# Token mixing one tile later, and softmax sums as a 65th column of the values, in a fused attention and mixer kernel

## The chip, the core and the metric

The kernel runs on one core of a Trainium2 chip. The core has five engines that run their own instruction queues: TensorE (PE: matmuls, with weight loads as PEld), VectorE (DVE), ScalarE (ACT), GpSimd (POOL) and SyncE (SP, which issues DMAs). They wait for each other by semaphores. The metric is the device time of one execution in microseconds.

## The reference

The inputs are q, k and v of 8 batches, 8 heads, 576 positions and 64 dimensions, and four weight matrices. Attention has a causal window of 64 positions. Its output x (576 x 512 a batch) goes through token mixing, a residual, channel mixing and another residual:

```
scores = where(0 <= i - j < 64, q @ k.T / 8, -1e9)
attn   = exp(scores - max);  attn = attn / (sum(attn) + 1e-9);  x = attn @ v
h   = relu(x.T @ w_tok1) @ w_tok2          # w_tok1 576x256, w_tok2 256x576
u   = x + h.T
out = u + relu(u @ w_ch1) @ w_ch2          # w_ch1 512x1536, w_ch2 1536x512
```

The weights come in float64 and are converted on the chip.

## The kernel before

The kernel has two stages. The first does attention and token mixing and ends near 284 us; the second does channel mixing in nine chunks of 512 tokens (lines L593 and L629).

The first stage works in 36 tiles, nine for a pair of batches. A tile i has 128 query rows: two blocks of 64, of one batch, or of two batches in the fifth tile of a pair (i % 9 = 4). The program is written out by hand: one loop runs over i from -1 to 36, and an iteration holds work of several tiles, so that what waits for one engine stands beside what another does. In iteration i stand, in this order:

- `pt_transpose(i, 0)`: four PE transposes of the softmax numerators e of half the heads into a PSUM tile pp (L301), and an ACT copy of it to SBUF as pt (L303). In the first four iterations (`early`) the other half follows at once; later it stands after the pieces named below. PSUM has two banks for pp.
- `softmax(i+1, 0)`: on DVE, the mask and the row maximum of the next tile's scores s (L283, L286; from tile 7 on). In the first tiles the mask is put in by PE (L260) and DVE takes only the maximum (L280, L281).
- `recip(i)`: sum + 1e-9, and its reciprocal ri (L321, L322, on DVE).
- `job_finish`: the halves of a converted weight; ACT makes the high half (L91), POOL or DVE the low one (L94).
- `softmax_exp(i+1, 0)`: four ACT exponentials with `accum_out` (L294), each with an instruction that reads the accumulator to give the row sums.
- a piece of token mixing's second matrix product, `tok2` (L393 transposes of x, L400 six matmuls), into the one bank "up", copied by ACT as u (L405).
- `job_convert_a`: DVE bit operations that turn float64 words to float32 (L185 to L188), in iterations whose number isn't divisible by three (and in the first six).
- `pt_transpose(i, 1)`, `softmax(i+1, 1)`.
- `tok1(n)` for the tiles n that a plan lists: the first token-mixing product h (L358), from three matmuls for each of two output halves, with x split in a high and a low part, xhi (ACT, L91) and xlo (POOL, L94). In the fifth tile of a pair the parts are made by half the rows (L338, L339). When a batch is complete, `finish_h` makes hhi (ACT, L369) and hlo (DVE, L370), and lists eight pieces.
- `softmax_exp(i+1, 1)`, `job_convert_b` (DVE, L197 to L200, and POOL, L202).
- `av(i)`: 32 matmuls xp = pt.T @ v (L313), and `norm(i)`: x = xp * ri (DVE, L327).
- `qk(i+2)`: scores of the tile after the next (L266), another piece, then `split_x` for tiles that the plan lists for the next iteration and that were not split yet.

The plan lists tile 0 in iteration 2, tile 1 in 3, tiles 2 and 3 in 4, and from then on tile i-1 in iteration i. So xhi and xlo of a tile are made between its `norm` and the first h matmuls of the next iteration.

PSUM has eight banks of 128 x 512 float32: s 2, pp 2 (tag "pt"), up 1, h 2, xp 1 (tag "av"). In the second stage these tags serve the products gp and op. The two functions of the plan and of the bank choice are in the lines below:

```
m = min(n + (1 if i < TOK1_SLOW else 2), i)          # L458
gp = ps.tile(..., tag=("s", "pt")[ft % 2])           # L589
tag, bufs = (("h", 2), ("av", 1), ("h", 2), ("up", 1))[ct]   # L617
```

Of the kernel before, what the change touches and what calls it, by code (L numbers as in the profile page):

```python
# [10 lines left out]
F32 = mybir.dt.float32  # L11
# [8 lines left out]

B, H, S, D = 8, 8, 576, 64
C = H * D
P = 128
BLK = 64
NBLK = S // BLK
# [2 lines left out]
NT = NPAIR * TPP  # L28
# [12 lines left out]


JOBS = {i: 1 if i < 6 or i % 3 else 0 for i in range(-1, 37)}
PIECES = {32: (1, 0), 33: (1, 0), 34: (1, 0), 35: (3, 0), 36: (2, 1)}

TOK1_FROM, TOK1_SLOW, TOK2_FROM = 2, 4, 7

N_PE, N_EARLY = 7, 4

# [25 lines left out]
def mixer_kernel(ctx: ExitStack, tc: tile.TileContext, qh, kh, vh, wt1, wt2, wc1, wc2, out):  # L75
# [37 lines left out]
    with ExitStack() as actx:  # L113
# [19 lines left out]
            loaded[i] = [qr, None]  # L133

        def load_v(i):
            vt = pq.tile([P, 2, H, D], F32, name=f"v{i}", tag="v", bufs=3)
            nc.sync.dma_start(vt, vh[i])
            loaded[i][1] = vt

# [129 lines left out]

        def softmax(i, u):  # L270
            if u == 0:
                st[i] = (pa.tile([P, H], F32, name=f"nm{i}", tag="nm", bufs=3),
                         pa.tile([P, H], F32, name=f"sum{i}", tag="sum", bufs=3))
            nm, sm = st[i]
            mk = mask[1 if tile_blocks(i)[0][1] == 0 else 0]
            e = pa.tile([P, 4, P], F32, name=f"e{i}_{u}", tag="e", bufs=4)
            e_sb[i, u] = e
            nmu = nm.rearrange("p (j u) -> p j u", u=2)[:, :, u]
            if i < N_PE:
                nc.vector.tensor_reduce(out=nmu, in_=s_ps[i, u], axis=AX.X, op=ALU.max, negate=True)  # L280
                nc.vector.tensor_scalar_mul(nmu, nmu, scale)  # L281
                return
            nc.vector.scalar_tensor_tensor(  # L283
                out=e, in0=s_ps.pop((i, u)), scalar=scale,
                in1=mk.unsqueeze(1).to_broadcast([P, 4, P]), op0=ALU.mult, op1=ALU.add)
            nc.vector.tensor_reduce(out=nmu, in_=e, axis=AX.X, op=ALU.max, negate=True)  # L286

        def softmax_exp(i, u):
            e = e_sb[i, u]
            nm, sm = st[i]  # L290
            src, by = (s_ps.pop((i, u)), scale) if i < N_PE else (e, 1.0)
            for h in range(4):
                g = 2 * h + u
                nc.scalar.activation(e[:, h], src[:, h], AF.Exp, bias=nm[:, g:g + 1], scale=by,  # L294
                                     accum_out=sm[:, g:g + 1])

        def pt_transpose(i, u):
            pp = ps.tile([P, 4, P], F32, name=f"pp{i}_{u}", tag="pt")
            e = e_sb.pop((i, u))
            for h in range(4):  # L300
                nc.tensor.transpose(pp[:, h], e[:, h], ident)  # L301
            pt = pa.tile([P, 4, P], F32, name=f"pt{i}_{u}", tag="ptsb", bufs=4)
            nc.scalar.copy(pt, pp)  # L303
            return pt
# [2 lines left out]

        def av(i, pts):
            vt = loaded.pop(i)[1]
            xp = ps.tile([P, H, D], F32, name=f"xp{i}", tag="av", bufs=1)  # L310
            for h in [*range(0, H, 2), *range(1, H, 2)]:
                for half in range(2):
                    nc.tensor.matmul(xp[half * BLK:(half + 1) * BLK, h],  # L313
                                     pts[h % 2][:, h // 2, half * BLK:(half + 1) * BLK],
                                     vt[:, half, h], start=True, stop=True)
            return xp

        def recip(i):
            _, sm = st.pop(i)
            ri = pa.tile([P, H], F32, name=f"ri{i}", tag="ri", bufs=2)  # L320
            nc.vector.tensor_scalar_add(ri, sm, 1e-9)  # L321
            nc.vector.reciprocal(ri, ri)  # L322
            return ri

        def norm(i, xp, ri):
            x = pa.tile([P, H, D], F32, name=f"x{i}", tag="x", bufs=12)
            nc.vector.tensor_mul(x, xp, ri.unsqueeze(2).to_broadcast([P, H, D]))  # L327
# [85 lines left out]
        def store_u():  # L413
            while stores:
                us, g0, n = stores.pop(0)
                a = 0
                while a < n:
# [2 lines left out]
                    (nc.sync if g0 < (B - 1) * S - 320 else nc.scalar).dma_start(u_dram[j][:, :, o:o + m], us[:, :, a:a + m])  # L420
                    a += m

        def tok1(i):
            p, t = divmod(i, TPP)
            b0, b1 = 2 * p, 2 * p + 1
            if t < 4:
                tok1_part(i, b0, full, t, t == 0, False)
            elif t == 4:
                tok1_part(i, b0, top, 4, False, True)
                finish_h(b0)  # L430
            else:
                if t == 5:
                    tok1_part(i - 1, b1, bottom, 4, True, False)
                tok1_part(i, b1, full, t - 5, False, t == 8)
                if t == 8:
                    finish_h(b1)

        def run_pieces(k):
            for _ in range(min(k, len(pieces))):
# [15 lines left out]
        load_v(1)  # L455
        tok1_plan, n = {}, 0
        for i in range(TOK1_FROM, NT + 1):
            m = min(n + (1 if i < TOK1_SLOW else 2), i)  # L458
            tok1_plan[i] = range(n, m)
            n = m  # L460
        qk(0)
        for i in range(-1, NT + 1):
            if 0 <= i and i + 2 < NT:
                load_v(i + 2)
            if 3 <= i + 3 < NT:
                load_q(i + 3)
            if i + 4 < NT:
                load_k(i + 4)
            store_u()
            n_jobs = JOBS[i]  # L470
            if i == NT - 1:
                up_tags += [("s", 2), ("pt", 2)]
# [36 lines left out]
            if i + 1 < NT:  # L509
                softmax_exp(i + 1, 1)  # L510
            for _ in range(n_jobs):
                job_convert_b()
            if 0 <= i < NT:
                xp = av(i, pts)
                if i + 1 < N_EARLY:
                    normed = [(i, xp, ri)]
# [22 lines left out]
    with ExitStack() as bctx:  # L539
# [45 lines left out]
        for j in range(NCHUNK):  # L585
            uf, uhi, ulo = ul.pop(j)
            g = []
            for ft in range(NFT):
                gp = ps.tile([P, CHUNK], F32, name=f"gp{j}_{ft}", tag=("s", "pt")[ft % 2])  # L589
                k = 0  # L590
                for ct in range(NCT):
                    for w, x in ((w1hi, uhi), (w1hi, ulo), (w1lo, uhi)):
# [19 lines left out]
            for ct in range(NCT):  # L612
                if j == 0:
                    for _ in range(7):
                        next(late, None)
                    assert all(n in finished for n in range(23 + 4 * ct, 27 + 4 * ct))
                tag, bufs = (("h", 2), ("av", 1), ("h", 2), ("up", 1))[ct]  # L617

                n_part = LAST_PARTS if j == NCHUNK - 1 and ct == NCT - 1 else 1
                for part in range(n_part):  # L620
                    cols = slice(part * CHUNK // n_part, (part + 1) * CHUNK // n_part)
                    if part:
                        tag, bufs = ("s", "pt")[part % 2], 2
# [47 lines left out]
```

## Time and profile before

| | |
|---|---|
| median of 3 runs | 878.97 us (878.91 to 879.26) |
| the profiled execution | 880.53 us, span 878.7 us, granted clock 0.993 |
| PE busy | 850.6 us (97% of the span) |
| PEld busy | 702.6 us (80%) |
| DVE busy | 378.3 us (43%) |
| ACT busy | 307.5 us (35%) |
| POOL busy | 105.3 us (12%) |
| mean duration of an exp, 128x128 | 396 ns; of the read of its accumulator 193 ns |

Times of the trace are counted from the start of the span. A row of the waits names the engine and the line that waited, and what released it, with the sum in us, the count and the longest. A row of the timeline has its start, its duration, the engine and line, the operation with out<-in, and in brackets the idle time before it. Busy times of PE are modelled: matmuls overlap, so the pace is read from start to start. ACT and DVE are idle for most of the second stage, so their shares of the span say little about the first.

### The profile page before, as it was taken

The page shows a single profiled execution, that of the slowest core. Times are in us where ns is not written, and L with a number is a line of the kernel's source. Part 1 is how long each engine was busy: PE and PEld are TensorE (multiplying, and loading weights), DVE is VectorE, ACT ScalarE, POOL GpSimd, SP SyncE. Part 2 cuts the span into 40 slices and gives each one's busy share as a digit, 9 for nine tenths or more (in the row PEclk, how much of TensorE's full clock was granted, in tenths as well). Part 3 has the DMA queues.
Part 4 walks back from the last instruction along what each step waited for, and adds up shares of the span by engine and source line. Part 5 has one row for each costly group of instructions (what it writes and reads, how often), then busy time and mean ns, then how long its engine had stood idle before and what let it go on. Part 6 is the DMA issues. An engine that isn't in the chain of part 4 may idle for free.

```text
span 878.7 us, 14566 instructions
## 1 busy us (share of the span) xinstructions
PE 850.6 (97%) x6002; PEld 702.6 (80%) x6002; DVE 378.3 (43%) x701; ACT 307.5 (35%) x966; POOL 105.3 (12%) x109
## 2 busy tenths in 40 slices
PE   6889999989989999999999999999999999999998
PEld 4668878868879878888888888888888888888887
DVE  5979878878874795220220220220220220220211
ACT  5778777878875341120120220220220220220200
POOL 3433343433332000000000000000000000000000
PEclk9989999999999999999999999999999999999999
DMA  9566667567535531100100100100100101100001
GB/s 322 195 203 229 200 235 244 183 235 246 182 127 167 182 106 57 60 7 30 60 13 24 60 13 25 60 13 25 60 12 31 54 13 39 46 13 37 0 13 37
DMA packets 39907, 84.69 MB, mean 96 GB/s; under 512 B 5281, under 2 KB 18337, under 8 KB 37921
## 3 DMA queue, kind: packets, MB, share of 16 engines
q1 hardware_dynamic: 37728, 81.93, 27.9%
q10 hardware_dynamic: 2112, 1.84, 0.6%
q8 instruction: 47, 0.77, 0.4%
q14 instruction: 20, 0.16, 0.1%
HBM read 64.09 MB, written 19.66 MB: 95 GB/s over the span
## 4 chain that ended last, share of the span: by engine, by line
PE 83%; DVE 8%; ACT 4%; POOL 2%; issue 2%; DMA 1%; POOLq 0%; SPq 0%; DVEq 0%; ACTq 0%
PE op L629 33%; PE gp L593 30%; PE h L358 5%; PE up L400 4%; PE s L266 4%; PE xp L313 3%; PE up L393 2%; POOL xlo L94 2%; PE pp L301 1%; ACT u L405 1%; DVE r L200 1%; DMA u_dram<-u 1%; DVE c L197 1%; ACT xhi L91 1%; ACT e L294 1%
## 5 line engine op out<-in xcount | busy, mean ns | idle before, releaser
L597 ACT ACTIVATE ghi<-gp 128x512 fp32r<-128x512 f32 x108 | 64.5, 597 | 432.2 <-PE gp L593 431.9
L629 PE MATMUL op<-ghi,w2lo 128*128 128x512 f32 (+1 forms) x444 | 170.9, 385 | 1.9 <-DVE w2lo L94 1.9
L629 PE MATMUL op<-glo,w2hi 128*128 128x512 f32 (+1 forms) x444 | 170.9, 385 | 0.0
L629 PE MATMUL op<-ghi,w2hi 128*128 128x512 f32 (+1 forms) x444 | 170.8, 385 | 0.0
L593 PE MATMUL gp<-ulo,w1hi 128*128 128x512 f32 x432 | 168.1, 389 | 0.0
L593 PE MATMUL gp<-uhi,w1hi 128*128 128x512 f32 x432 | 168.1, 389 | 0.0
L593 PE MATMUL gp<-uhi,w1lo 128*128 128x512 f32 x432 | 168.0, 389 | 0.0
L598 DVE SCALAR_TENSOR_TENSOR glo<-gp,ghi 128x512 fp32r<-128x512 f32 x108 | 74.5, 690 | 187.7 <-ACT ghi L597 187.7
L631 DVE TENSOR_TENSOR uf<-op,uf 128x512 f32<-128x512 f32 (+1 forms) x37 | 25.0, 677 | 243.7 <-PE op L629 243.7
L629 PEld LDWEIGHTS op<-ghi,w2lo 128*128 128x128 f32 x444 | 83.9, 189 | 18.8 <-DVE w2lo L94 2.3
L629 PEld LDWEIGHTS op<-ghi,w2hi 128*128 128x128 f32 x444 | 83.8, 189 | 16.6
L629 PEld LDWEIGHTS op<-glo,w2hi 128*128 128x128 f32 x444 | 83.8, 189 | 16.5
L593 PEld LDWEIGHTS gp<-uhi,w1hi 128*128 128x128 f32 x432 | 81.1, 188 | 16.9
L593 PEld LDWEIGHTS gp<-uhi,w1lo 128*128 128x128 f32 x432 | 81.1, 188 | 16.8
L593 PEld LDWEIGHTS gp<-ulo,w1hi 128*128 128x128 f32 x432 | 81.1, 188 | 16.8
L294 ACT ACTIVATE e<-e,nm 128x128 f32<-128x128 f32 x232 | 90.5, 396 | 8.0 <-DVE nm L286 8.0
L94 POOL TENSOR_TENSOR xlo<-x,xhi 128x512 fp32r<-128x512 f32 x32 | 42.9, 1340 | 66.3 <-ACT xhi L91 66.0
L313 PEld LDWEIGHTS xp<-v,pt 128*64 128x64 f32 x1152 | 37.4, 137 | 16.4 <-ACT pt L303 6.3
L266 PE MATMUL s<-k,q 64*64 64x128 f32 x1152 | 43.7, 287 | 2.4 <-DVE c L197 1.9
L313 PE MATMUL xp<-v,pt 128*64 128x64 f32 x1152 | 43.1, 226 | 2.7 <-ACT pt L303 2.4
L294 ACT ACTIVATION_READ_ACCUMULATOR e<-e,nm 128x1 f32 x232 | 44.8, 193 | 0.0
L303 ACT COPY pt<-pp 128x512 f32<-128x512 f32 x72 | 41.8, 587 | 6.4 <-PE pp L301 6.3
(79 smaller groups left out, 1002.7 us busy)
## 6 DMA issues: line engine op xcount, KB each, us to landing
v<-vh SPq DMA_DIRECT2D x36, 512.0 KB, 3.8
raw<-wc SPq DMA_DIRECT2D x32, 384.0 KB, 4.4
q<-qh SPq DMA_DIRECT2D x36, 256.0 KB, 4.6
k<-kh SPq DMA_DIRECT2D x7, 1280.0 KB, 8.0
out<-uf SPq DMA_DIRECT2D x35, 256.0 KB, 2.3
uf<-u_dram SPq DMA_DIRECT2D x8, 1024.0 KB, 5.6
u_dram<-u SPq DMA_DIRECT2D x7, 512.0 KB, 3.7
k<-kh SPq DMA_DIRECT2D x5, 256.0 KB, 6.2
```

Source lines behind the costliest of these rows:

```text
L94: eng_lo.tensor_sub(lo, src, hi.bitcast(F32))
L266: nc.tensor.matmul(s[u][half * BLK:(half + 1) * BLK, j], qt[r, j, half], kbs[b][r, j, n * BLK:n * BLK + P], start=not on_pe, stop=True, sk ...
L294: nc.scalar.activation(e[:, h], src[:, h], AF.Exp, bias=nm[:, g:g + 1], scale=by, accum_out=sm[:, g:g + 1])
L303: nc.scalar.copy(pt, pp)
L313: nc.tensor.matmul(xp[half * BLK:(half + 1) * BLK, h], pts[h % 2][:, h // 2, half * BLK:(half + 1) * BLK], vt[:, half, h], start=True, sto ...
L358: nc.tensor.matmul(h_ps[b][tt], w[:, o + tt * P:o + (tt + 1) * P], x, start=first and n == 0, stop=last and n == len(combos) - 1)
L400: nc.tensor.matmul(up[:, :n], hx[:, cs], w[:, tt * S + s0:tt * S + s0 + n], start=False, stop=(k == 6), skip_group_check=True)
L593: nc.tensor.matmul(gp, w[:, ct * F + ft * P:ct * F + (ft + 1) * P], x[:, ct], start=(k == 0), stop=(k == 3 * NCT - 1))
L597: nc.scalar.activation(ghi, gp, AF.Relu)
L598: nc.vector.scalar_tensor_tensor(out=glo, in0=gp, scalar=0.0, in1=ghi.bitcast(F32), op0=ALU.max, op1=ALU.subtract)
L629: nc.tensor.matmul(op, w[:, ct, ft], x[:, cols], start=(k == 0), stop=(k == 3 * NFT - 1))
L631: nc.vector.tensor_add(uf[:, ct, cols], op, uf[:, ct, cols])
```

## The change

Two things are changed at once.

The plan of `tok1` lags one tile more: up to iteration 33, iteration i handles tiles up to i-2; in iteration 34 two tiles are done, and from there the plan is as before. The halves of x(i) are thus made in iteration i+1, behind its first pt copy, and used in iteration i+2. `finish_h` is moved from within `tok1` behind `av` and `norm`. One more piece is run in iteration 34.

The row sums no longer come from the accumulator. The host puts v in rows of 66 per head: 64 values, a 1 and a 0. `av` multiplies 65 of them, so column 64 of xp is the row sum. xp takes two PSUM banks, four heads in each. `norm` reads the sums from xp, adds 1e-9, takes the reciprocal and multiplies. For the second xp bank, pp has one bank instead of two. In the second stage gp takes banks of s and h, and op those of av, pt, up and av.

```diff
-PIECES = {32: (1, 0), 33: (1, 0), 34: (1, 0), 35: (3, 0), 36: (2, 1)}
-TOK1_FROM, TOK1_SLOW, TOK2_FROM = 2, 4, 7
+PIECES = {32: (1, 0), 33: (1, 0), 34: (2, 0), 35: (3, 0), 36: (2, 1)}
+TOK1_FROM, TOK1_SLOW, TOK1_CATCH_UP, TOK2_FROM = 2, 4, 34, 7
...
-            vt = pq.tile([P, 2, H, D], F32, name=f"v{i}", tag="v", bufs=3)
+            vt = pq.tile([P, 2, H, DV], F32, name=f"v{i}", tag="v", bufs=3)
...
-                nc.scalar.activation(e[:, h], src[:, h], AF.Exp, bias=nm[:, g:g + 1], scale=by,
-                                     accum_out=sm[:, g:g + 1])
+                nc.scalar.activation(e[:, h], src[:, h], AF.Exp, bias=nm[:, g:g + 1], scale=by)
...
-            pp = ps.tile([P, 4, P], F32, name=f"pp{i}_{u}", tag="pt")
+            pp = ps.tile([P, 4, P], F32, name=f"pp{i}_{u}", tag="pt", bufs=1)
...
-            xp = ps.tile([P, H, D], F32, name=f"xp{i}", tag="av", bufs=1)
+            xp = ps.tile([P, 2, CHUNK], F32, name=f"xp{i}", tag="av", bufs=1)
+            xp = xp[:, :, :4 * (D + 1)].rearrange("p u (j d) -> p u j d", j=4)
...
-                    nc.tensor.matmul(xp[half * BLK:(half + 1) * BLK, h],
+                    nc.tensor.matmul(xp[half * BLK:(half + 1) * BLK, h % 2, h // 2],
                                      pts[h % 2][:, h // 2, half * BLK:(half + 1) * BLK],
-                                     vt[:, half, h], start=True, stop=True)
+                                     vt[:, half, h, :D + 1], start=True, stop=True)
...
-        def recip(i):
-            _, sm = st.pop(i)
-            ri = pa.tile([P, H], F32, name=f"ri{i}", tag="ri", bufs=2)
-            nc.vector.tensor_scalar_add(ri, sm, 1e-9)
+        def norm(i, xp):
+            ri = pa.tile([P, 2, 4], F32, name=f"ri{i}", tag="ri", bufs=2)
+            nc.vector.tensor_scalar_add(ri, xp[:, :, :, D], 1e-9)
             nc.vector.reciprocal(ri, ri)
-            nc.vector.tensor_mul(x, xp, ri.unsqueeze(2).to_broadcast([P, H, D]))
+            nc.vector.tensor_mul(x.rearrange("p (j u) d -> p u j d", u=2), xp[:, :, :, :D],
+                                 ri.unsqueeze(3).to_broadcast([P, 2, 4, D]))
...
-                finish_h(b0)
+                to_finish_h.append(b0)
...
-            m = min(n + (1 if i < TOK1_SLOW else 2), i)
+            m = min(n + (1 if i < TOK1_SLOW else 2), i - (i < TOK1_CATCH_UP))
...
-            if 0 <= i < NT:
-                ri = recip(i)
...
-                    norm(i, xp, ri)
+                    norm(i, xp)
+            while to_finish_h:
+                finish_h(to_finish_h.pop(0))
...
-                gp = ps.tile([P, CHUNK], F32, name=f"gp{j}_{ft}", tag=("s", "pt")[ft % 2])
+                gp = ps.tile([P, CHUNK], F32, name=f"gp{j}_{ft}", tag=("s", "h")[ft % 2])
...
-                tag, bufs = (("h", 2), ("av", 1), ("h", 2), ("up", 1))[ct]
+                tag, bufs = (("av", 1), ("pt", 1), ("up", 1), ("av", 1))[ct]
```

What it does to the order shows in tile 22. ScalarE's queue before, from the cast of x(21) to the exponentials of the second half (the numbers behind names are those of buffers, e_0 and e_1 the halves of tile 23):

```order
L91 CAST xhi_2692<-x_2661 128x512
L303 COPY pt_0_2705<-pp_0_2700 128x512
L294 ACTIVATE e_0_2709,sum_2708<-e_0_2709,nm_2707 128x128 x4
L405 COPY u_1_2622<-up_1_2_2719 128x320
L303 COPY pt_1_2739<-pp_1_2734 128x512
L294 ACTIVATE e_1_2741,sum_2708<-e_1_2741,nm_2707 128x128 x4
```

And now, the same stretch of ScalarE's queue:

```order
L304 COPY pt_0_2649<-pp_0_2644 128x512
L94 CAST xhi_2655<-x_2609 128x512
L296 ACTIVATE e_0_2652<-e_0_2652,nm_2651 128x128 x4
L405 COPY u_1_2673<-up_1_0_2663 128x320
L304 COPY pt_1_2684<-pp_1_2679 128x512
L296 ACTIVATE e_1_2686<-e_1_2686,nm_2651 128x128 x4
```

The cast of x(21) stands behind the first pt copy instead of ahead of it, and the exponentials have no sums. VectorE's queue before, around `norm(21)`:

```order
L286 TENSOR_REDUCE nm_2598<-e_1_2631 128x4
L327 TENSOR_TENSOR x_2661<-xp_2644,ri_2603 128x512
L283 SCALAR_TENSOR_TENSOR e_0_2709<-s_0_2663,mask_89 128x512
L286 TENSOR_REDUCE nm_2707<-e_0_2709 128x4
L321 TENSOR_SCALAR ri_2712<-sum_2599 128x8
L322 RECIPROCAL ri_2712<-ri_2712 128x8
```

And now:

```order
L288 TENSOR_REDUCE nm_2545<-e_1_2576 128x4
L323 TENSOR_SCALAR ri_2606<-xp_2589 128x8
L324 RECIPROCAL ri_2606<-ri_2606 128x8
L326 TENSOR_TENSOR x_2609<-xp_2589,ri_2606 128x2x4x64
L285 SCALAR_TENSOR_TENSOR e_0_2652<-s_0_2611,mask_89 128x512
```

The sum and its reciprocal stand directly ahead of the product x, and read xp. On TensorE, the iteration with four h matmuls and no piece between the transposes is 24 (and 15) now; it was 23 (and 32):

```order
L302 MATMUL pp_0_2887<-ident,e_0_2772 128x128 x4
L302 MATMUL pp_1_2908<-ident,e_1_2809 128x128 x4
L358 MATMUL h_0_2464<-xhi_2777,t1hi 128x512
L358 MATMUL h_0_2464<-xhi_2777,t1z 128x512
L358 MATMUL h_1_2465<-xhi_2777,t1hi 128x512
L358 MATMUL h_1_2465<-xhi_2777,t1z 128x512
L316 MATMUL xp_2926<-v_2639,pt_0_2892 64x65 x8
L316 MATMUL xp_2926<-v_2639,pt_1_2913 64x65 x8
```

The two groups of transposes pp stand next to each other there, and share one bank; the values' matmuls stream 65 columns.

More of the change, by code (lines that the diff above doesn't have):

```diff
@@ L22 @@
 C = H * D
+DV = D + 2
 P = 128
@@ L271, in softmax @@
             if u == 0:
-                st[i] = (pa.tile([P, H], F32, name=f"nm{i}", tag="nm", bufs=3),
-                         pa.tile([P, H], F32, name=f"sum{i}", tag="sum", bufs=3))
-            nm, sm = st[i]
+                st[i] = pa.tile([P, H], F32, name=f"nm{i}", tag="nm", bufs=3)
+            nm = st[i]
             mk = mask[1 if tile_blocks(i)[0][1] == 0 else 0]
@@ L289, in softmax_exp @@
             e = e_sb[i, u]
-            nm, sm = st[i]
+            nm = st.pop(i) if u else st[i]
             src, by = (s_ps.pop((i, u)), scale) if i < N_PE else (e, 1.0)
@@ L421, in store_u @@
                     a += m
+        to_finish_h = []
         def tok1(i):
@@ L435, in tok1 @@
                 if t == 8:
-                    finish_h(b1)
+                    to_finish_h.append(b1)
         def run_pieces(k):
@@ L471, in mixer_kernel @@
             if i == NT - 1:
-                up_tags += [("s", 2), ("pt", 2)]
+                up_tags += [("s", 2), ("pt", 1)]
             have = len(pieces)
@@ L515, in mixer_kernel @@
                 if i + 1 < N_EARLY:
-                    normed = [(i, xp, ri)]
+                    normed = [(i, xp)]
                 else:
-                    norm(i, xp, ri)
+                    norm(i, xp)
+            while to_finish_h:
+                finish_h(to_finish_h.pop(0))
             if i + 2 < NT:
@@ L622, in mixer_kernel @@
                     if part:
-                        tag, bufs = ("s", "pt")[part % 2], 2
+                        tag, bufs = "s", 2
                     op = ps.tile([P, CHUNK], F32, name=f"op{j}_{ct}_{part}", tag=tag, bufs=bufs)[:, cols]
@@ L648 @@
     vw = np.stack([vb[bi, ji], vb[bi, ji + 1]], 2).reshape(NT, 2, P, H, D)
-    vh = vw.transpose(0, 2, 1, 3, 4)
+    vh = np.zeros((NT, P, 2, H, DV), v.dtype)
+    vh[..., :D], vh[..., D] = vw.transpose(0, 2, 1, 3, 4), 1
     wt1, wt2, wc1, wc2 = (np.ascontiguousarray(inputs["moe_w_" + n]).view(np.int64)
```

2 lines of the change are left out of this document (removed).

## The prediction

> **What bounds the kernel now.** I read the table of windows first, then the queue waits of TensorE's weight loads, then one tile in order of time. The windows (columns: busy us of PE, PEld, DVE, ACT, POOL, each with its count; granted clock, DMA share, GB/s):
>
> ```profile
> 0.00:50.00 50.00, 38.08 (x510) 27.52 (x510) 36.61 (x85) 34.24 (x134) 21.96 (x38) 1.00 0.77 272
> 50.00:100.00 50.00, 47.47 (x605) 39.42 (x604) 43.61 (x83) 38.44 (x147) 17.94 (x16) 0.93 0.60 199
> 150.00:200.00 50.00, 46.42 (x640) 37.83 (x639) 41.65 (x79) 39.22 (x151) 19.83 (x17) 1.00 0.61 204
> 400.00:878.00 478.00, 475.31 (x2131) 394.85 (x2130) 93.55 (x140) 62.66 (x108) 0.00 (x0) 1.00 0.09 31
> ```
>
> From 400 us on TensorE never rests (475.31 of 478), and the change leaves that stage its instructions. What can move is the attention stage, up to about 284 us. In its middle PE is 93% busy (46.42 of 50), DVE 83%, ACT 78%: PE leads, and small stalls inside each tile are all there is to win. The first 50 us are different: PE 76%, DVE 73% of a stretch that also has the start in it. The stalls from 60 to 255 us (27 tiles, 6 to 32):
>
> ```profile
> 60.00:255.00 195.00, 186.10 (x2504) 153.43 (x2501) 161.63 (x308) 154.07 (x580) 75.11 (x64) 1.00 0.65 218
> PEld h L358 <- POOL xlo L94: 8.0, 17, 1.2
> PEld up L393 <- ACT u L405: 6.3, 22, 0.3
> PEld h L358 <- POOL xhi L339: 4.4, 3, 2.0
> PEld xp L313 <- ACT pt L303: 4.3, 11, 0.9
> PEld h L358 <- ACT xhi L91: 0.8, 2, 0.4
> ```
>
> Token mixing (h) waits 13.2 us (8.0 + 4.4 + 0.8) for the halves of x, which POOL makes; attention times values (xp) waits 4.3 us for the copied transposes. The up wait, 0.3 us a tile, is the one PSUM bank of token mixing's second half. Tile 22 in time:
>
> ```profile
> 170.46 0.60 PE L301 MATMUL pp<-ident,e 128*128 128x128 f32 x4
> 170.63 0.16 DVE L321 TENSOR_SCALAR ri<-sum 128x8 f32<-128x8 f32 x1
> 170.98 0.62 ACT L91 CAST xhi<-x 128x512 fp32r<-128x512 f32 x1
> 171.50 0.59 ACT L303 COPY pt<-pp 128x512 f32<-128x512 f32 x1
> 171.68 1.52 POOL L94 TENSOR_TENSOR xlo<-x,xhi 128x512 fp32r<-128x512 f32 x1 [5.08 <-ACT xhi L91]
> 171.98 0.41 ACT L294 ACTIVATE e<-e,nm 128x128 f32<-128x128 f32 x1
> 172.41 0.60 PE L301 MATMUL pp<-ident,e 128*128 128x128 f32 x4
> 172.76 0.48 PE L358 MATMUL h<-xhi,t1hi 128*128 128x512 f32 x1
> 173.25 0.50 PE L358 MATMUL h<-xlo,t1hi 128*128 128x512 f32 x1
> 173.82 0.39 PE L358 MATMUL h<-xhi,t1hi 128*128 128x512 f32 x1
> 174.05 0.39 PE L358 MATMUL h<-xlo,t1hi 128*128 128x512 f32 x1
> 174.60 1.01 PEld L313 LDWEIGHTS xp<-v,pt 128*64 128x64 f32 x32 [0.35 <-ACT pt L303]
> ```
>
> The second matmul of h starts 0.49 us after the first, where 0.23 is the pace (173.82 to 174.05), since xlo ends at 173.20.
>
> **The change, part by part.** *Two tiles behind.* From tile 4 on, the halves of x(i) are made in iteration i+1, and used in i+2; xlo has a tile's time (some 7 us) more. All 13.2 us of waits go: −13.2. Nothing takes their place on the h matmuls, since even behind both ACT casts and a POOL pass of 1.5 us xlo is done in the iteration before.
>
> *Softmax sums.* The read of the accumulator goes from ScalarE:
>
> ```profile
> L294 ACT ACTIVATE e<-e,nm 128x128 f32<-128x128 f32 x232 | 90.5, 396 | 8.0 <-DVE nm L286 8.0
> L294 ACT ACTIVATION_READ_ACCUMULATOR e<-e,nm 128x1 f32 x232 | 44.8, 193 | 0.0
> L313 PE MATMUL xp<-v,pt 128*64 128x64 f32 x1152 | 43.1, 226 | 2.7 <-ACT pt L303 2.4
> L321 DVE TENSOR_SCALAR ri<-sum 128x8 f32<-128x8 f32 x36 | 11.5, 321 | 0.0
> L322 DVE RECIPROCAL ri<-ri 128x8 f32<-128x8 f32 x36 | 7.3, 203 | 1.2
> ```
>
> Now one exp and its read take 0.39 us from start to start. No row shows exps without reads; the spacing is at least 0.20 (396 − 193 ns) and at most 0.39. In tile 22 two ACT operations back to back overlap by 0.10 us (xhi starts at 170.98, lasts 0.62, and pt starts at 171.50), so I take 0.30: 0.36 us less for four exps. The cast of x, however, moves from ahead of the first copy pt to behind it, 0.52 us in front of the exps and the second pt. So the second pt comes no earlier in tiles with both casts and earlier in the others: of the 4.3 us of xp waits I count half, −2.2. The Trainium skill, "ScalarE: Activation LUTs", section "What ACT_TABLE_LOAD costs", gives an ACTIVATE with a pointer bias 280 ns + 0.833 N, overlapping the next by 93 ns: an estimate of 0.29 us at N = 128. By it the sum would stay as it is, since ACT is not the bound.
>
> *The 65th column.* 1152 matmuls of 43.1 us stream 65 columns for 64: +0.7 (43.1/64). No row has an odd count; the bounds are 0 and, were they to cost double, the 1.08 us of a tile's 32 matmuls again (39 us in all, a rival).
>
> *Reciprocal behind the values.* The same two DVE instructions now wait for xp and stand ahead of x, 0.36 us (0.16 + 0.20, where nothing holds them). Behind them on DVE stands the next e from s, which today waits 0.33 us for PE anyway (the third row is for the next part):
>
> ```profile
> 175.80 0.69 DVE L327 TENSOR_TENSOR x<-xp,ri 128x512 f32<-128x512 f32 x1 [0.91 <-PE xp L313]
> 176.82 0.69 DVE L283 SCALAR_TENSOR_TENSOR e<-s,mask 128x512 f32<-128x512 f32 x1 [0.33 <-PE s L266]
> 177.98 1.04 PE L301 MATMUL pp<-ident,e 128*128 128x128 f32 x8
> ```
>
> So it is covered; only in the last tile, where x feeds the last h directly, +0.4. The wider v is 3% more bytes in a queue at a share of 0.65: 0. finish_h behind the values sends hhi and hlo later, but the next iteration's scores and transposes lie ahead of their use: 0, at most 0.3 in eight places.
>
> *One bank for pp.* The second transposes now wait for the first pt copy. In most tiles a piece (transposes and six matmuls, 1.3 us) lies between: in tile 22 the copy ended 0.32 us ahead (171.50 + 0.59 against 172.41), and with the cast behind it the copy starts some 0.4 us sooner. Tiles 15 and 24 have no piece between: first four transposes 0.60, copy 0.59, hand-overs 0.1 before the second four start, against 0.44 now (eight take 1.04, four 0.60): 0.85 each, +1.7. Before tile 7 there is no piece either, but there DVE is what ends last.
>
> *Before 60 us.* The chain of waits runs through DVE alone from the first to the second row here; at tiles 4 to 6 it goes through ACT, as the rows of the timeline behind them show:
>
> ```profile
> 18.63 0.70 DVE nm L280
> ...
> 37.72 0.61 DVE x L327
> ```
>
> ```profile
> 47.12 1.36 DVE L94 TENSOR_TENSOR t2lo<-w,t2hi 128x384 fp32r<-128x384 f32 x1 [1.30 <-ACT t2hi L91]
> 50.44 0.37 ACT L294 ACTIVATE e<-s,nm 128x128 f32<-128x128 f32 x1 [0.48 <-DVE nm L281]
> 52.00 1.97 PE L266 MATMUL s<-k,q 64*64 64x128 f32 x28 [1.92 <-DVE c L197]
> 56.09 0.63 PE L358 MATMUL h<-xlo,t1z 128*128 128x512 f32 x1
> ```
>
> t2hi now stands ahead of the casts of x, so DVE's 1.30 us goes; four exps of PE's next scores are 0.4 us shorter; ten h matmuls leave tiles 4 to 6, some of them at a lower clock (0.63 us each, not 0.39). Bounds 0 and −6; I take −3, nearest the first two. Those ten matmuls are done later, where PE is the bound: 10 × 0.23 = +2.3.
>
> Sum: −13.2 − 2.2 + 0.7 + 0.4 + 1.7 − 3 + 2.3 = −13.3. The profiled execution took 880.53 us (span 878.7), 1.6 above the median 878.97; 880.5 − 13.3 − 1.6 = 865.6, so 866.
>
> **Rivals.**
> *DVE takes over* (16 in 100, 874). POOL's passes move to where DVE does the second half of a conversion. While POOL works, DVE's operations from SBUF to SBUF stretch:
>
> ```profile
> 264.68 0.60 DVE L321 TENSOR_SCALAR ri<-sum 128x8 f32<-128x8 f32 x1
> 265.55 1.35 POOL L94 TENSOR_TENSOR xlo<-x,xhi 128x512 fp32r<-128x512 f32 x1 [0.29 <-DVE ri L322]
> 265.78 1.33 DVE L187 TENSOR_SCALAR c<-c 128x384 f32<-128x384 f32 x1
> 260.96 0.36 DVE L188 TENSOR_SCALAR c<-c 128x384 int32<-128x384 int32 x1
> ```
>
> 1.33 against 0.36. DVE has (195 − 161.63)/27 = 1.2 us a tile to spare, 0.5 of which the faster PE takes back. One more such stretch (0.97) in the 18 converting tiles leaves 0.3 to 0.5 us a tile exposed, 5 to 8 us: 871 to 874. Against it: the sums in PSUM free L321, and PE needs DVE's results a tile later only. The Trainium skill, "SBUF — State Buffer", section "SBUF: two separate sides", says that VectorE and GpSimd share a port pair as an exclusive lock for the whole instruction; the rows agree.
>
> *The single bank holds PE in every tile* (8 in 100, slower, 889). If ACT starts the first copy late, behind u or a w1hi that waits for POOL, the second transposes wait for it. Fully exposed it is 0.85 us in 27 tiles, +23, so 866 + 23. It decides from 0.5 us a tile (13.3/27); the 0.3 to 0.7 us between copy and transposes speak against it.
>
> *The 65th column is dear* (3 in 100): 866 + 38 = 904. Nothing in the profile speaks for it.
>
> *Everything clears* (13 in 100): all 4.3 us of xp waits, and 6 before 60 us: 858 to 861.
>
> **How the numbers follow.** Forecast 60 in 100, its own range 862 to 870. A measurement tells 0.2% (1.8 us) from no change. Faster: 60 + 13 + 11 of the 16 of DVE = 84; same: 4, DVE's worst case; slower: 8 + 3 + 1 of DVE = 12. The range 858 to 876 leaves out the slower rivals and little else.
>
> **What would show it.** Right: no wait of h on POOL between 60 and 255 us; ACT busy some 25 us lower or more with the reads gone; xp's matmuls at 226 ns still; waits of pp on pt in tiles 15 and 24 alone; tiles near 6.9 us. Wrong: pp waiting on ACT pt in most tiles, xp L316 slower than by 1/64, DVE without idle time, or a lower granted clock than now.

## The result, and the profile after

The changed kernel takes 883.39 us (881.95 to 885.51) where the kernel before takes 879.01 us beside it: a ratio of 1.0047, with a 95% interval of 1.0028 to 1.0065. It is 4.4 us slower, where 13 us less were forecast. The profiled execution took 883.87 us (span 882.0, granted clock 0.994).

The windows of the changed kernel, in the columns explained above:

```profile
0.00:50.00 50.00, 37.67 (x469) 26.77 (x470) 35.05 (x80) 26.57 (x75) 19.85 (x37) 1.00 0.75 251
50.00:100.00 50.00, 45.89 (x597) 37.80 (x599) 42.13 (x78) 33.39 (x92) 17.73 (x15) 0.90 0.62 206
150.00:200.00 50.00, 48.16 (x668) 40.37 (x661) 42.44 (x81) 36.24 (x98) 18.76 (x16) 1.00 0.69 226
400.00:881.00 481.00, 478.58 (x2146) 397.57 (x2144) 93.60 (x140) 62.65 (x108) 0.00 (x0) 1.00 0.09 31
```

In the middle TensorE is busier than before (48.16 of 50, against 46.42), as forecast. The second window is the opposite: 45.89 against 47.47, and a clock of 0.90 against 0.93. Where the time went is read from the starts of the values' matmuls (the first xp of a tile) and of the first gp. I call the stretches by tiles:

| stretch, profiled execution (us) | before | after | difference | forecast |
|---|---|---|---|---|
| start to tile 7 | 64.7 | 69.3 | +4.6 | −3 |
| tile 7 to tile 32 | 183.4 | 178.4 | −4.9 | −10.7 (−13.2 − 2.2 + 1.7 + 0.7 + 2.3) |
| tile 32 to the first gp | 35.3 | 40.7 | +5.4 | +0.4 |
| first gp to the end | 595.3 | 593.6 | −1.7 | 0 |

So a gain is there, less than half of what was forecast, and both ends of the first stage eat it. Some of it is moved work: six h matmuls leave the first stretch, two of them go to the second and four to the third, and one piece goes from the second to the third. With 0.23 us for a matmul and 1.1 us for a piece (53.1 us for 47 of them before, in the table below), 2.0 us of the third stretch's 5.4 are work. The last row has no step of the change behind it: the execution of before that was profiled ran 3.4 us at half clock at 324 us, this one did not. The other choice of banks in the second stage costs nothing there: from its 200th matmul to its 2400th it takes 498.7 us in both profiles.

The waits of the changed kernel from 60 to 255 us, the six largest rows of TensorE on h, xp, pp and s:

```profile
PEld xp L316 <- issue: 6.3, 17, 0.4
...
PEld xp L316 <- ACT pt L304: 3.7, 9, 0.6
...
PEld xp L316 <- DVE c L200: 2.6, 7, 0.4
PE xp L316 <- ACT pt L304: 2.3, 7, 0.4
PEld pp L302 <- ACT pt L304: 1.9, 2, 1.0
PE pp L302 <- ACT pt L304: 1.5, 2, 0.7
```

No row has h waiting for POOL: all of the 13.2 us are gone. The groups:

```profile
PE 852.3 (97%) x6002; PEld 705.5 (80%) x6002; DVE 379.9 (43%) x701; ACT 283.1 (32%) x678; POOL 105.3 (12%) x109
L296 ACT ACTIVATE e<-e,nm 128x128 f32<-128x128 f32 x232 | 74.3, 394 | 14.8 <-DVE nm L288 14.7
L316 PE MATMUL xp<-v,pt 128*64 128x65 f32 x1152 | 47.1, 232 | 4.5 <-ACT pt L304 4.3
```

ACT lost 24.4 us (307.5 to 283.1), and the exps wait longer for DVE (14.7, before 8.0). To see what a wait is worth, I summed for tiles 7 to 32 the time from each PE matmul's start to the next one's, by what the matmul makes (up with its transposes):

| us, tiles 7 to 32 | h | xp | pp | s | up | sum |
|---|---|---|---|---|---|---|
| before | 46.3 | 29.2 | 28.9 | 25.9 | 53.1 | 183.4 |
| after | 40.3 | 32.3 | 26.2 | 27.2 | 52.5 | 178.4 |

h is 6.0 us faster, not 13.2, and xp 3.1 us slower. That h was worth 6 stood in the same view of the kernel before, in the rows of PE itself, which the prediction did not use:

```profile
PE h L358 <- POOL xhi L339: 3.7, 3, 1.7
PE h L358 <- POOL xlo L94: 2.4, 5, 0.9
```

3.7 + 2.4 = 6.1. The rows of PEld are waits in the queue of weight loads; while a weight load waits, earlier matmuls still run. The Trainium skill, "TensorE: Matmul & The Clock Gate", section "Step-by-step: what each phase is for", says that TensorE pulls weight loads ahead of the matmuls in flight, and the two sums (13.2 and 6.1) agree with that.

### The profile page after: what moved, and what is told of

Its sections match the earlier page's. It is cut to its first block, busy times and chain, and to the rows that moved or that the text cites. A ratio compares the mean times of both kernels' runs of the same rounds, so it can differ in the third digit from the quotient of the medians.

```text
span 882.0 us, 14325 instructions
## 1 busy us (share of the span) xinstructions
PE 852.3 (97%) x6002; PEld 705.5 (80%) x6002; DVE 379.9 (43%) x701; ACT 283.1 (32%) x678; POOL 105.3 (12%) x109
## 4 chain that ended last, share of the span: by engine, by line
PE 77%; DVE 15%; ACT 3%; issue 2%; DMA 2%; SPq 0%; POOLq 0%; POOL 0%; DVEq 0%; ACTq 0%
PE op L631 33%; PE gp L595 30%; PE up L400 4%; PE h L358 3%; PE xp L316 3%; PE s L269 2%; PE up L393 2%; DVE e L285 2%; PE pp L302 2%; DVE nm L288 1%; DVE c L190 1%; DVE r L203 1%; DVE c L200 1%; ACT e L296 1%; DVE c L191 1%
## 5 line engine op out<-in xcount | busy, mean ns | idle before, releaser
L296 ACT ACTIVATE e<-e,nm 128x128 f32<-128x128 f32 x232 | 74.3, 394 | 14.8 <-DVE nm L288 14.7
L316 PEld LDWEIGHTS xp<-v,pt 128*64 128x64 f32 x1152 | 39.8, 142 | 20.1 <-issue 7.7
L302 PE MATMUL pp<-ident,e 128*128 128x128 f32 x288 | 46.3, 285 | 7.0 <-ACT pt L304 6.5
L316 PE MATMUL xp<-v,pt 128*64 128x65 f32 x1152 | 47.1, 232 | 4.5 <-ACT pt L304 4.3
L269 PE MATMUL s<-k,q 64*64 64x128 f32 x1152 | 45.8, 291 | 3.0 <-ACT e L296 1.8
```

The lines of the kernel that those rows point to most:

```text
L269: nc.tensor.matmul(s[u][half * BLK:(half + 1) * BLK, j], qt[r, j, half], kbs[b][r, j, n * BLK:n * BLK + P], start=not on_pe, stop=True, sk ...
L316: nc.tensor.matmul(xp[half * BLK:(half + 1) * BLK, h % 2, h // 2], pts[h % 2][:, h // 2, half * BLK:(half + 1) * BLK], vt[:, half, h, :D + ...
```

## The experiments

Each kernel below ran five to twelve times beside the kernel before (878.6 to 879.0 us there). The stretches are those of the first table, from each profile. A profile shows a single execution, so a difference of a microsecond or two between stretches can be that execution's own.

| kernel | median us | ratio, 95% interval | to tile 7 | 7 to 32 | 32 to gp | rest |
|---|---|---|---|---|---|---|
| before | 879.01 | 1 | 64.7 | 183.4 | 35.3 | 595.3 |
| after | 883.39 | 1.0028–1.0065 | 69.3 | 178.4 | 40.7 | 593.6 |
| lag alone | 889.22 | 1.0094–1.0133 | 66.9 | 183.0 | 42.0 | 595.4 |
| ones alone | 890.22 | 1.0113–1.0152 | 70.8 | 184.5 | 40.3 | 593.5 |
| one pp bank | 890.23 | 1.0103–1.0141 | 70.2 | 184.6 | 39.0 | 594.6 |
| finish_h early | 887.78 | 1.0069–1.0112 | 67.8 | 180.8 | 42.0 | 596.3 |
| casts late | 880.36 | 1.0008–1.0026 | 64.4 | 179.5 | 42.2 | 592.4 |
| early banks | 881.66 | 1.0030–1.0062 | 65.1 | 178.1 | 40.7 | 592.9 |
| tail as before | 880.98 | 1.0018–1.0040 | 68.8 | 180.0 | 38.0 | 592.5 |
| three together | 876.00 | 0.9968–0.9988 | 61.8 | 182.2 | 38.0 | 592.3 |
| casts late in early tiles | 874.55 | 0.9927–0.9958 | 61.8 | 179.2 | 38.0 | 592.0 |
| the same, no early banks | 875.74 | 0.9942–0.9969 | 64.0 | 179.2 | 38.0 | 592.3 |
| lag alone, mended | 877.56 | 0.9974–0.9994 | 62.0 | 183.8 | 35.2 | 594.2 |
| ones alone, early banks | 888.72 | 1.0093–1.0128 | 67.3 | 186.0 | 40.2 | 595.9 |

**The parts apart.** First theories: A, the single bank of pp costs, the lag gains; B, the lag itself costs. The first kernel is the one before with the lag, the late finish_h and the second piece of iteration 34, with accumulators and two pp banks (the lines of finish_h are not shown):

```diff
-PIECES = {32: (1, 0), 33: (1, 0), 34: (1, 0), 35: (3, 0), 36: (2, 1)}
+PIECES = {32: (1, 0), 33: (1, 0), 34: (2, 0), 35: (3, 0), 36: (2, 1)}
-            m = min(n + (1 if i < TOK1_SLOW else 2), i)
+            m = min(n + (1 if i < TOK1_SLOW else 2), i - (i < 34))
...
```

> The kernel before with the lag alone (token mixing two tiles behind, finish_h behind the values, two pieces in iteration 34); the sums still come from the accumulators, pp keeps two banks and xp one. Theory A (the single bank of pp, which the second bank of xp forces, is what costs): no loss in the first tiles, the waits of h on POOL gone as in the changed kernel, so faster than before: 873 to 877 us. Theory B (the lag itself costs, by the casts of x ahead of the exponentials and by the late hlo in the last tiles): slower than before, 880 to 884 us, with xp waiting for pt in nearly every tile.

The second is the changed kernel with the lag, the second piece of iteration 34 and finish_h taken back:

```diff
-            m = min(n + (1 if i < TOK1_SLOW else 2), i - (i < TOK1_CATCH_UP))
+            m = min(n + (1 if i < TOK1_SLOW else 2), i)
...
-                to_finish_h.append(b0)
+                finish_h(b0)
...
```

> The changed kernel with the lag taken back (plan, pieces and finish_h as before); the column of ones, two banks for xp and one for pp stay. Theory A: the first four tiles lose some 4 us as in the changed kernel, the waits of h on POOL are back, the shorter exponentials give 1 to 3 us: 880 to 884 us. Theory B: the same as before within 0.2%, 877 to 881 us.

The third is the kernel before with one pp bank and the bank choice of the second stage of after:

```diff
-            pp = ps.tile([P, 4, P], F32, name=f"pp{i}_{u}", tag="pt")
+            pp = ps.tile([P, 4, P], F32, name=f"pp{i}_{u}", tag="pt", bufs=1)
...
```

> The kernel before with pp in one bank and nothing else changed (the bank that comes free is used by nobody in the first stage; the banks of the second stage as in the changed kernel). Theory A: 4 to 6 us slower than before, 883 to 885 us, of which 3 to 4 by the time tile 3's values start. Theory B: within 0.2% of before, 878 to 881 us, since DVE hides the wait.

They took 889.22, 890.22 and 890.23 us: no theory had any of them above 885. Each part alone costs 10 to 11 us, and both together 4.4. The parts are not terms of a sum; each takes away some of what the other costs.

What the lag costs without the column of ones is in the waits of that kernel from 60 to 255 us:

```profile
PEld xp L313 <- ACT pt L303: 12.0, 21, 1.8
PE xp L313 <- ACT pt L303: 8.6, 15, 1.7
```

The row of PE was 1.1 before and is 2.3 after. The cast of x now stands on ACT between the first pt copy and the exps. With accumulator reads, four exps take 1.55 us (from 174.51 to the next ACT instruction at 176.06, in the iteration of tile 22), and the second pt copy behind them comes late; xp took 39.6 us in tiles 7 to 32 and gave back all that h gained (40.1). Without reads four exps take 1.28 us (a row for it stands further down), and most of that wait goes.

What the single bank costs without the lag is in tile 4 of the ones-alone kernel:

```profile
38.01 1.52 DVE L200 SCALAR_TENSOR_TENSOR c<-raw,c 128x384 int32<-128x384 int32 x1
...
39.19 0.66 PE L302 MATMUL pp<-ident,e 128*128 128x128 f32 x4
...
40.94 0.69 DVE L326 TENSOR_TENSOR x<-xp,ri 128x512 f32<-128x512 f32 x1
41.67 0.62 ACT L94 CAST xhi<-x 128x512 fp32r<-128x512 f32 x1 [2.97 <-DVE x L326]
42.19 0.58 ACT L304 COPY pt<-pp 128x512 f32<-128x512 f32 x1
42.83 0.82 PE L302 MATMUL pp<-ident,e 128*128 128x128 f32 x4 [2.98 <-ACT pt L304]
```

The first transposes are done at 39.85, but without the lag the cast xhi stands ahead of the pt copy on ACT, and waits for x, which DVE makes behind a weight conversion. With two banks the second transposes don't care; with one they wait 2.98 us for x. From 60 to 255 us the same kernel has "pp <- ACT pt" in PEld's queue seven times, 9.8 us, where after has it twice, 1.9. The lag moves that cast behind the copy: the wait of tile 4 is 0.73 us in after, so the lag is what makes the single bank bearable.

**finish_h.** The changed kernel with finish_h back within tok1:

```diff
-                to_finish_h.append(b0)
+                finish_h(b0)
...
-                    to_finish_h.append(b1)
+                    finish_h(b1)
```

> The changed kernel with finish_h back within tok1, ahead of the values. Theory A and B alike: the wait of up on ACT in iteration 34 (2.6 us) goes, since hlo no longer stands ahead of e on DVE: 880 to 882 us. If the tail is late for another reason (the sixteen h matmuls of iteration 34), it stays at 883.

It took 887.78 us, 4.4 more than after: its late place, costed at nothing, is a gain. The theory failed in its mechanism too: the wait of up on ACT in iteration 34 is still there (2.6 us in PE's row), and the stretch from tile 32 on takes 42.0 us. The stretch to tile 7 is 1.5 us shorter with finish_h early, the other three together 6.3 longer. Of these, 2.7 lie behind the first gp, and 1.7 of them are lost in 3.4 us at half clock at 332.6 us, which the profile of after does not have; so part of the gain is the clock's, and its size is open. Why it is a gain was not followed further.

**Three places.** The next theory: the loss of after is in three places, each with its own cause. First, the casts of x ahead of the exps. This kernel makes them at the end of the iteration:

```diff
-            for n in tok1_plan.get(i + 1, ()):
-                last_use = n - NX + ((n - NX) % TPP == 4)
-                if n < i and last_use not in tok1_plan.get(i, ()):
-                    split_x(n)
```

> The changed kernel, with the halves of x(i-1) cast at the end of iteration i, behind the scores and the piece, not in iteration i ahead of the exponentials. Theory A: in the steady tiles the values' matmuls (xp) wait for the second pt copy because ACT's casts now stand ahead of the exponentials. Then xp of tiles 7 to 32 goes from 32.3 us start to start back to 28 to 30, with h still free of POOL, and the time is 879 to 881. Theory B: xp waits for another reason (the one pp bank, or DVE that takes the reciprocal ahead of the next mask): xp stays at 32 and the time at 882 to 885; if POOL's halves come late again, h goes back from 40 to 43 us or more.

It took 880.36 us, A's number, but not by A's way. xp came back to 28.6 us, and h and pp gave it up again (43.4 and 29.0, after 40.3 and 26.2): steady tiles took 179.5, not less than after. The gain is in tiles 4 to 7, 20.5 us where after has 26.2. DVE and POOL in after:

```profile
49.93 1.43 POOL L339 TENSOR_TENSOR xhi<-x,xhi 64x512 fp32r<-64x512 f32 x1 [1.20 <-issue]
50.25 1.32 DVE L190 TENSOR_SCALAR c<-c 128x384 f32<-128x384 f32 x1
51.43 1.27 POOL L339 TENSOR_TENSOR xlo<-x,xlo 64x512 fp32r<-64x512 f32 x1
51.61 1.31 DVE L191 TENSOR_SCALAR c<-c 128x384 int32<-128x384 int32 x1
53.81 1.15 ACT L296 ACTIVATE e<-s,nm 128x128 f32<-128x128 f32 x4 [1.73 <-DVE nm L283]
55.01 1.97 PE L269 MATMUL s<-k,q 64*64 64x128 f32 x28 [1.83 <-ACT e L296]
```

and the same two DVE operations and the scores with the casts late:

```profile
49.45 0.36 DVE L190 TENSOR_SCALAR c<-c 128x384 f32<-128x384 f32 x1
49.84 0.36 DVE L191 TENSOR_SCALAR c<-c 128x384 int32<-128x384 int32 x1
52.30 1.09 PE L269 MATMUL s<-k,q 64*64 64x128 f32 x28 [0.65 <-ACT e L296]
```

POOL's halves of x(4) fall on the conversion of the token weights. DVE's two operations end 0.2 us behind POOL's two (1.32 and 1.31 us, not 0.36), the maximum and the exps come late, the scores wait 1.83 us, and 28 of them take 1.97 us instead of 1.09, since the clock has fallen to half (10.2 us from 54.2 on; with the casts late 3.4 us, from 54.8 on, behind these scores). The Trainium skill, "SBUF — State Buffer", section "SBUF: two separate sides", describes the lock of a port pair by which one of the two engines blocks for the other's whole instruction; the rows agree. The same kernel also takes ACT's two casts of x(4) (0.62 us each, from 49.18 on in after) from in front of the exps and the second pt copy, on which the values' matmuls waited 0.93 us there. What the collision and these casts are worth each was not run apart.

Second, the one bank in the first tiles. Here the second half of pp has banks of h and up that are idle there:

```diff
-            pp = ps.tile([P, 4, P], F32, name=f"pp{i}_{u}", tag="pt", bufs=1)
+            tag, bufs = {0: ("h", 2), 1: ("h", 2), 2: ("up", 1), 5: ("up", 1), 6: ("up", 1)}.get(i, ("pt", 1)) if u else ("pt", 1)
+            pp = ps.tile([P, 4, P], F32, name=f"pp{i}_{u}", tag=tag, bufs=bufs)
```

> The changed kernel, with the second half of pp in a bank of its own in tiles 0, 1, 2, 5 and 6 (banks of h and up that are idle there); one bank for both halves remains in tiles 3, 4 and from 7 on. Theory A: in the first tiles the single bank is what costs, by its waits and by a clock gate that opens some 6 us later: tile 3's values start near 33.5 us instead of 36.5, the clock is full from about 14 us, and the time is 878 to 881. Theory B: the start is late for another reason (the wider values, the sums read from xp): tile 3 still starts above 35.5 us and the time is 882 to 885.

In the profile most of the early loss is gone, nearer to A than to B: tile 3 starts at 34.2 us (after 36.5, before 32.8), tile 7 at 65.1 (69.3). In after:

```profile
15.65 1.12 PE L302 MATMUL pp<-ident,e 128*128 128x128 f32 x4 [0.68 <-ACT pt L304]
16.69 2.00 PE L316 MATMUL xp<-v,pt 128*64 128x65 f32 x32
22.28 0.66 PE L302 MATMUL pp<-ident,e 128*128 128x128 f32 x4 [0.68 <-ACT pt L304]
```

and with the early banks:

```profile
13.94 1.64 PE L303 MATMUL pp<-ident,e 128*128 128x128 f32 x8
15.72 1.21 PE L317 MATMUL xp<-v,pt 128*64 128x65 f32 x32
```

The wait of 0.68 us a tile is gone in these tiles, and so is the half clock at that place: 32 matmuls in 1.21 us, not 2.00. The unprofiled runs don't confirm a gain, though: 881.66 us with a spread from 878.61 (the profiled one) to 885.14, and an interval that is nearly that of after. Their granted clocks lie between 0.988 and 0.997. By the time it is open; the pair further down tells more.

Third, the tail: the catch-up in iteration 32, and the second piece there instead of in 34.

```diff
-PIECES = {32: (1, 0), 33: (1, 0), 34: (2, 0), 35: (3, 0), 36: (2, 1)}
+PIECES = {32: (1, 1), 33: (1, 0), 34: (1, 0), 35: (3, 0), 36: (2, 1)}
-TOK1_FROM, TOK1_SLOW, TOK1_CATCH_UP, TOK2_FROM = 2, 4, 34, 7
+TOK1_FROM, TOK1_SLOW, TOK1_CATCH_UP, TOK2_FROM = 2, 4, 32, 7
```

> The changed kernel, with the lag of token mixing ended in iteration 32 instead of 34 (tiles 30 and 31 there), and one piece in iteration 34, as before the change. Theory A: iteration 34, with two tiles of h and a second piece that waits for its bank, is what lengthens the end of the stage: from tile 32's values to the first gp it takes 35 to 37 us instead of 40.7, and the time is 878 to 880. Theory B: the end is longer whatever the place of the catch-up, since the last tiles have the sums and the late finish of h ahead of e on VectorE: 40 us or more, and 882 to 885.

It took 880.98 us: 38.0 us from tile 32 on, between A and B in the profile, and 1.5 us more in the tiles before. Of the 2.7 us by which the end is shorter, 0.9 are four h matmuls that now stand in the tiles before. The rest is roughly the wait of the second piece for its bank in iteration 34 of after, 2.57 us, less a new wait of 1.1 us of up on pt. The rows of after:

```profile
258.47 1.28 ACT L296 ACTIVATE e<-e,nm 128x128 f32<-128x128 f32 x4 [1.39 <-DVE nm L288]
259.65 0.35 ACT L405 COPY u<-up 128x256 f32<-128x256 f32 x1
260.06 0.44 PE L393 MATMUL up<-ident,x 128*128 128x128 f32 x2 [2.57 <-ACT u L405]
```

The copy that frees the one bank up is queued on ACT behind exps that wait for DVE.

> The three edits at once (casts at the end of the iteration, early banks, catch-up in iteration 32). Theory A: the three losses are in three places and add up: 883.4 - 3 - 4 - 4 = 872, between 870 and 875, below the kernel before. Theory B: what is won early is waited back later (by the weights' conversion on VectorE or the loads): 877 to 882.

It took 876.00 us: below the kernel before, and 1 us above the range of A. In the first stretch 7.4 us are won, of the 4.8 and 4.2 that its two edits had won apart; in the tail all 2.7; but the steady tiles took 182.2.

**A version that beats both.** So the late casts should pay early and cost later. The same kernel, with late casts only up to iteration 7:

```diff
-                if n < i and last_use not in tok1_plan.get(i, ()):
+                if n < i and i > 7 and last_use not in tok1_plan.get(i, ()):
```

> The three edits of the run before, but with the casts of x at the end of the iteration only up to iteration 7; from iteration 8 on they stand ahead of the exponentials again, as in the changed kernel. Theory A: the late casts pay only where the token weights are converted (tiles 4 to 6), and later they only move waits from xp to h and pp: tiles 7 to 32 take 179 to 180 us instead of 182, and the time is 873 to 875. Theory B: the place of the casts doesn't matter later: 876 as before.

It took 874.55 us, ratio 0.9942 (0.9927 to 0.9958), as A has it, with 179.2 us in the steady tiles: 4.2 us below the kernel before beside it, and 8.8 below the median of after. (The two profiles lie 7.7 us apart, since that of before is 1.5 us above the 879.01 of the table and this one 1.7 below its median. 3.3 of the 7.7 lie behind the first gp: 1.7 are lost in the 3.4 us at half clock of before, and 1.7 in a wait of the first op for a converted weight, 1.86 us before and 0.12 here.) Its first windows:

```profile
0.00:50.00 50.00, 38.42 (x518) 27.99 (x522) 36.03 (x89) 28.86 (x83) 19.09 (x37) 1.00 0.78 271
50.00:100.00 50.00, 48.16 (x675) 39.73 (x666) 42.79 (x81) 36.36 (x99) 21.18 (x18) 1.00 0.62 208
```

675 matmuls stand between 50 and 100 us where after has 597, and the clock is full.

The same without the early banks:

> The kernel beside it, with one bank for pp in all tiles. Theory A: the single bank costs in the first tiles: tile 3's values start above 35.5 us, not near 34.5, the clock opens fully some 3 to 5 us later, and the time is 2 to 4 us above that of the kernel beside it. Theory B: what the first tiles lose is taken back by tile 7, where the weights' conversion on VectorE is behind anyway: within 1 us of it.

Tile 3 starts at 36.2 us instead of 34.4, and the 2.2 us that it is behind at tile 7 are still there at the end of the profile (873.5 against 871.0), but the medians are only 1.2 us apart, between A and B, and the intervals overlap. So by the profile the single bank costs some 2 us in the first tiles; by the time, no more than that.

The lag alone (the first kernel) with the casts at the end of the iteration and the catch-up in iteration 32:

> The lag alone (sums by the accumulator, two banks of pp), with the casts at the end of the iteration and the catch-up in iteration 32. Theory A: the lag alone cost 10 us because its casts stood between the first pt copy and exponentials that with their accumulator reads are too long to leave room, and because of the last tiles: mended, xp goes from 39.6 to 29 to 31 us in tiles 7 to 32 and the time from 889 to 877 to 880. Theory B: the lag costs for another reason: 884 or more.

It took 877.56 us, 11.7 less than unmended and 1.1 less than before beside it; xp is back at 30.4. A was right in the time and in xp. But the steady tiles took 183.8 us, no less than before: the mended lag gains ahead of tile 7 (62.0 us against 64.7), not by the waits of h. h waits for POOL again in part: PE's two rows, 6.1 before, are 3.5 here.

```profile
PE h L358 <- POOL xhi L339: 3.1, 2, 1.6
PE h L358 <- POOL xlo L94: 0.4, 2, 0.2
```

And the column of ones alone with the early banks:

> The column of ones alone, with the second half of pp in idle banks in tiles 0, 1, 2, 5 and 6. Theory A: the single bank of the first tiles is most of what the column of ones costs: from 890.2 to 884 to 886. Theory B: the column costs for other reasons (the sums read behind the values, the bank in later tiles): 888 or more.

It took 888.72 us, as B has it. The banks cover tiles 0, 1, 2, 5 and 6, but the long waits, 3.25 us in tile 4 and six of 7.2 us together from 60 to 255 us, are where one bank is left, and they remain.

## Why the prediction was wrong, point by point

The mechanism that was forecast for token mixing came true, and so did most of its signs: no wait of h on POOL, ACT less busy by nearly the 25 us asked for (24.4), waits of pp on pt from 60 to 255 us in tiles 15 and 24 alone. But these signs look at the steady tiles, and say nothing of the size. The steady tiles gained 4.9 us, not 10.7 (7.1 us a tile, where 6.9 were asked for), and the first tiles and the last lost 10.0 where the sum had them at −2.6.

- *The waits of h, −13.2.* All of the waits went. Their price was wrong: it was summed from PEld's rows, and PE's own rows (6.1) and the starts of the matmuls (6.0) give less than half. This is an error of 7.2 us in the sum. It is softened by pp, which became 2.7 us shorter in these tiles, unforeseen (the lag alone has that too, 24.5 after 28.9).
- *xp, −2.2.* It became +3.1. That the cast moves in front of the exps was seen and taken to cancel out, but it outweighs what the shorter exps save. Their spacing, 0.30 taken, is 0.30 (four in 1.28 us, 394 ns each).
- *One bank for pp.* +1.7 in tiles 15 and 24 was right: the two waits are 1.5 us in PE's row together. "Before tile 7 there is no piece either, but there DVE is what ends last" is the step that failed: in each of the tiles 0 to 6 the second transposes wait 0.7 us for the first copy, and with that the clock opens later (it is full from 20.1 us in after, from 15.1 with the early banks). The row of after from 0 to 60 us, which before does not have:

```profile
PE pp L302 <- ACT pt L304: 5.0, 7, 0.7
```

- *Before 60 us, −3.* It is +4.6 at tile 7, with 7.6 us the largest error. The bounds 0 and −6 had no loss in them, since a gain was all that was looked for. Two losses are found: the single bank (some 2 us by the profiles), and the halves of x that are now made during the conversion of the token weights (tiles 4 to 7 take 26.2 us; 22.9 before, 20.5 with the casts late). The prediction had the collision of POOL and DVE as its rival "DVE takes over" and placed it in the steady tiles: the mechanism is in the rows, the place was wrong, and the forecast of 874 with it. Tile 3 starts 1.4 us later than before even with the early banks; what that is stays open.
- *The last tiles, +0.4.* They are +5.4, of which 2.0 are moved work. For the two tiles and the second piece of iteration 34 the sum had no wait; the one bank up, freed by a copy behind exps that wait for DVE, cost 2.57 us there.
- *Ten h matmuls moved late, +2.3.* Six leave the stretch to tile 7, 1.4 us by the same price, and four of them come behind tile 32.
- *The 65th column, +0.7.* It is cheap, as forecast. A tile's 32 matmuls still go in 1.08 us (176.33 to the next scores at 177.41 in tile 22; before 174.60 to 175.68). The mean duration rose from 226 to 232 ns, but from 70 to 247 us only to 227; the rise is in the first tiles, where the clock is at half.
- *finish_h, 0.* Its late place is a gain, unforeseen: 4.4 us by the medians.
- *Rivals.* The rival of a single bank that holds PE in every tile did not come about: the bank waits in two steady tiles and in the first ones. Of the 12 in 100 for slower, 11 were on that and on a dear column; that several small things at both ends outweigh a gain was given none.

## What to carry to other kernels

Price a wait by the rows of PE itself and by matmul starts, not by the weight-load queue: here the two differed by a factor of two. When a change moves work on an in-order engine, list for the first, a steady and the last tiles what stands behind it there: the same cast of x made the values' matmuls of the middle tiles wait 10.4 us behind long exps and 3.1 behind short ones, it sent POOL's halves of x(4) into a weight conversion, and its place decided whether one PSUM bank was dear or cheap. And parts that seem to add up can each depend on the other: alone they cost 10 and 11 us, together 4.4, and with three small repairs they gain 4.2.

## What the runs showed of the hardware that was not expected

The granted clock falls after short waits. Its stretches at half are 3.4, 6.8 or 10.2 us long in these traces (after: 10.2 at 54 us; before: 6.8 at 51 us and 3.4 at 324), and the one at 54 us in after begins within the scores' wait of 1.83 us. A wait of that size does not always bring one: the 2.57 us in iteration 34 of after have none behind them, while with the casts late the same wait (2.56 us) is followed by 3.4 us at half clock. The best kernel has no such stretch from 17.3 us until the last matmuls. The Trainium skill, "TensorE: Matmul & The Clock Gate", section "What's actually happening", states that the clock falls to half after at least one idle window of about 3.4 us. The three lengths are one, two and three of these, but the traces do not bear out that a whole window must be idle: after the first 18 us no wait of TensorE in any of them reaches 3.4 us, and the longest is 3.25.

A stretch of 10.2 us at half clock is worth up to 4.6 us of matmul time, an estimate from the 28 scores that take 1.97 us there and 1.09 otherwise. That is as much as the whole difference between the two kernels. In their two profiles, though, the stretches at half behind the start add up to 10.2 us in each, and only the start differs: the clock is full from 20.1 us in after, from 13.8 before. Most other executions of before have a higher clock (0.996 to 0.998) than its profiled one (0.993), so how much of the difference is the clock's and how much that of the waits that bring it about was not told apart.

The spread of a kernel from execution to execution goes with the clock in part: the six runs with early banks have clocks of 0.988 to 0.997 and times of 885.1 to 878.6 us, nearly in that order. The six with the tail as before all have 0.994 and still lie 2.7 us apart.
